# The out stage of three token groups as seven block products, in a fused linear attention and bilinear FFN kernel

## The chip, the cores and the metric

The kernel runs on one core of a Trainium2 chip. The core has TensorE (matmuls, called PE in the profile), VectorE (DVE), ScalarE (ACT), GpSimd (POOL) and the DMA queues, here almost all of them issued by SyncE (SP). Each engine takes its own instructions in the order in which the program lists them, and waits at an instruction until what it needs is there. The metric is the device time of one execution in microseconds (us), as the median of several runs.

## The reference

An attention without softmax, in blocks with a decaying state, feeds a feed-forward layer of two products. Cut to what matters:

```python
# q, k, v: (4 batches, 8 heads, 768 positions, 64); block = 64; lam: one number per head
for b in range(nb):
    intra = (qb @ kb.T * Dmask) @ vb               # Dmask[i, j] = lam ** (i - j) for i >= j, else 0
    inter = (qb * lam_pow) @ kv_state
    out[block b] = intra + inter
    kv_state = lam ** block * kv_state + (kb * rev_pow).T @ vb
x = out as (3072 tokens, 512)
y = ((x @ w_a) * (x @ w_b)) @ w_out                # w_a, w_b: 512 x 1536; w_out: 1536 x 512
```

Everything comes in and goes out as fp32. The kernel computes its matmuls in bf16 with fp32 sums.

## The kernel before, in words

**Units and groups.** The attention works in 24 units of 128 tokens (six per batch). GROUPS (L28) gathers them into eight groups of 4, 1, 2, 4, 4, 4, 4 and 1 units for the feed-forward layer. While TensorE does the layer for one group, the attention of the next group's units is put between its matmuls.

**Attention of a unit.** q and k are scaled by powers of lam and cast to bf16 (`scale`, L317, mostly on GpSimd), transposed by the DMA engines (`dma_start_transpose`, L346) or, for units 4 to 6, on TensorE (`piece_T`); v is cast to bf16 (`make_vb`, on an engine that the table VB_ENG names). `piece_S` makes the scores kq = k q (L374) and `mask` multiplies them by a triangle on VectorE (L391). `pieces_O` sums state times q and v times masked scores into o_ps (L408); `evac_o` copies it as bf16 into xT (L431), the transposed input of the next group. `piece_V` and `kv_beside` bring the state up to date, and KV_ENG says who copies it. The first four units are packed together ahead of group 0.

**The order of the work.** PLAN (L43) is written out by hand. Each group's matmul loop calls `hook(slot)` at fixed points, and PLAN lists what is emitted there: T transpose, S scores, O output, V state, P (PK, PV) preparing a unit, C cast of a w_out chunk, WS a weight sum, X the x sums, W a store of an early output that was kept. `pump` (L230) issues loads on SP's queue, in one order, as far as buffers and LOOKAHEAD allow; transposes and stores are issued on the same queue.

**Weights.** Chunks of fp32 weights of 512 KB land in the pool wst (eight buffers of 4 KB per partition) and are cast to bf16 by `cast_w`. The same pool holds first q and k of units 0 to 3, later the kept outputs, and later still the fp32 copies and oab of the groups 3 to 6. Group 0 uses w_a and w_b in steps, as they land.

**Groups 3 to 6** (`ffn_z`, L625). Here the products x w_a and x w_b are made as 2 x 2 blocks with seven products instead of eight (the Strassen-Winograd scheme): sums of weight blocks are made once (`weight_sum`, on VectorE), sums of x blocks per group (`x_sums`, z_add, z_sub, z_mix, on VectorE). A loop over n = 0..5 (NP = 6 pairs of 128 columns of w_a and w_b) makes seven `product`s of four matmuls of 256 columns each, into the PSUM accumulators U, V and W; U alternates between banks 0 and 1, V between 2 and 3, W is in 4. An accumulator is used for more than one product, so in between ScalarE copies it away (`snap`, L647: u1, v1, u2) and later VectorE subtracts that copy from the accumulator into oab (L679, L688, L689). `finish` of pair n, called in iteration n + 1, adds the last product, has ScalarE copy U into oab (L656), and has VectorE multiply a by b into ab (L658).

**Out stage.** For these groups `out_part` multiplies ab by w_out: four tiles of 128 tokens, twelve chunks of 128 rows, 512 columns each, which is 48 matmuls (L697) per group. ScalarE copies each tile's result (L552) and SP stores it. Groups 0, 1, 2 and 7 go through `ffn` (L510 the products with w_a and w_b, L537 their product, L557 the out stage). Group 7 is one unit, and its output is stored in three parts at the end.

Of the kernel before, what the change touches and what calls it, by code (L numbers as in the profile page):

```python
# [22 lines left out]
def _bc(ap, dims):  # L23
# [8 lines left out]
W_BUFS = 8  # L32
# [10 lines left out]
PLAN = {  # L43
# [21 lines left out]
}  # L65
Z_GROUPS = (3, 4, 5, 6)
KV_ENG = dict(enumerate(["dve"] * 10 +
                        ["act"] * 2 +
                        ["dve"] +
                        ["act"] * 3 +  # L70
                        ["dve"] * 6 +
                        ["act"] +
                        ["dve"]))
VB_ENG = dict(enumerate(["pool"] * 7 +
                        ["dve"] * 3 +
                        ["act"] * 2 +
                        ["dve"] +
                        ["pool"] * 4 +
                        ["dve"] +
                        ["pool"] * 2 +  # L80
                        ["act"] +
                        ["dve"] +
                        ["pool"] * 2))
# [3 lines left out]
def kernel(  # L87
# [25 lines left out]
    wst_pool = ctx.enter_context(tc.tile_pool(name="wst", bufs=W_BUFS))  # L113
    ld_pool = ctx.enter_context(tc.tile_pool(name="ld", bufs=4))
    prep_pool = ctx.enter_context(tc.tile_pool(name="prep", bufs=6))
# [3 lines left out]
    a_pool = ctx.enter_context(tc.tile_pool(name="a", bufs=4))  # L119
# [5 lines left out]
    sum_pool = ctx.enter_context(tc.tile_pool(name="sum", bufs=1))  # L125
    ctx.enter_context(tc.manual_schedule())
# [24 lines left out]
    def load_x(w, u):  # L151
        b, nb = divmod(u, NB)
        t = ld_pool.tile([128, H, D], F32, name=w + "f", tag=w + "f")
        nc.sync.dma_start(out=t, in_={"q": qr, "k": kr, "v": vr}[w][b, nb])  # L154
        raw[u, w] = t
# [7 lines left out]
    staged = {}  # L163
    w_off = [sum(W_CHUNKS[:i]) for i in range(len(W_CHUNKS) + 1)]
# [7 lines left out]
    def load_w(kind, c):  # L172
        t = wst_pool.tile([128, 1024], F32, name="wst", tag="wst")
        if kind == "o":
            t = t[:].rearrange("p (k n) -> p k n", k=2)
# [8 lines left out]
        staged[kind, c] = t  # L184

    def cast_w(kind, c, eng):
        t = staged.pop((kind, c))
# [4 lines left out]
        if eng == "act":  # L192
            nc.scalar.copy(dst, t)
        elif eng == "first":
            nc.vector.tensor_copy(dst[:, :3, :128], t[:, :3, :128])
            nc.gpsimd.tensor_copy(dst[:, 3:, :128], t[:, 3:, :128])
            nc.gpsimd.tensor_copy(dst[:, :, 128:], t[:, :, 128:])
        else:
            nc.vector.tensor_copy(dst, t)  # L199
# [3 lines left out]
    wz = {kind: sum_pool.tile([128, 4, 2, HF], BF16, name="wz_" + kind, tag="wz_" + kind)  # L203
          for kind in "ab"}

    def weight_sum(i):
        kind, j = "ab"[i % 2], i // 2
        w, z = (wa_sb if kind == "a" else wb_sb), wz[kind]
        a11, a12 = w[:, 0:2, :HF], w[:, 2:4, :HF]
        a21, a22 = w[:, 0:2, HF:], w[:, 2:4, HF:]  # L210
        if j == 0:
            nc.vector.tensor_sub(z[:, 0], a22, a21)
        elif j == 1:
            nc.vector.tensor_sub(z[:, 1], a11, z[:, 0])
        elif j == 2:
            nc.vector.tensor_sub(z[:, 2], a12, z[:, 1])
        else:
            nc.vector.tensor_add(z[:, 3], a11, a21)
# [11 lines left out]
    def pump():  # L230
        while pending:
            kind, c = pending[0]
            if kind in "abo":
                if len(staged) >= W_BUFS:
                    return
# [8 lines left out]
    idle_sb = singles.tile([128, 512], BF16, name="idle_sb")  # L244
# [11 lines left out]

    x4 = {}
# [666 lines left out]
```

## Time and profile before

| | us |
|---|---|
| median of 3 runs | 228.15 (227.94 to 228.88) |
| profiled execution | 228.72 |
| its span, first to last instruction | 227.0 |
| TensorE busy in the span | 217.8 |
| VectorE, ScalarE, GpSimd busy | 154.6, 117.0, 59.2 |
| groups 3 to 6 in the span | 85.0 to 215.4 |

The 40 digits of a slice row are tenths of busy time in stretches of 5.7 us. The chain of waits follows the execution back from its last instruction, from each step to what released it; its columns are start, length, and engine, tile and line, with a number of instructions. Rows of instructions by tile give shortest, median and longest duration in ns. Matmuls are pipelined: each lasts longer (379 ns for 512 columns) than the distance to the next one (about 216 ns).

### The profile page before, as it was taken

What the parts mean: (1) busy time and instruction counts of PE and PEld (TensorE: products, weight loads), DVE (VectorE), ACT (ScalarE), POOL (GpSimd) and SP (SyncE); (2) the same over time, 40 slices, a digit from 0 to 9 for tenths busy, and PEclk for the clock granted to TensorE, in tenths of its full rate; (3) what the DMA queues carried; (4) which work ended last, traced back from release to release, by engine and by line L of the source; (5) the groups of instructions that cost most, each with busy time, mean ns of one, the idle gap of its engine ahead of it and who ended that gap; (6) DMA issues with size and microseconds to landing.
All of it is one profiled execution on the core that took longest, in us unless ns stands there. A gap on an engine that the chain in (4) does not pass through costs nothing.

```text
span 227.0 us, 5349 instructions
## 1 busy us (share of the span) xinstructions
PE 217.8 (96%) x2127; PEld 148.3 (65%) x2127; DVE 154.6 (68%) x257; ACT 117.0 (52%) x233; POOL 59.2 (26%) x73
## 2 busy tenths in 40 slices
PE   7798999999899999999999999999999999999994
PEld 2374444447678758877458887448887458885493
DVE  0994773969959868999356988676988318773050
ACT  2685465037443267656247685127576236672261
POOL 6061000147843254424424434460000000000000
PEclk9999999999999999999999999999999999999999
DMA  4999999999999999999999999943020030000311
GB/s 131 318 261 350 359 387 319 271 222 196 233 192 200 240 187 269 212 233 184 181 247 237 205 186 231 169 153 92 3 48 1 27 144 18 1 3 0 141 46 46
DMA packets 97544, 39.40 MB, mean 174 GB/s; under 512 B 85488, under 2 KB 92016, under 8 KB 97520
## 3 DMA queue, kind: packets, MB, share of 16 engines
q1 hardware_dynamic: 97232, 39.00, 80.4%
q8 instruction: 16, 0.26, 0.5%
q10 hardware_dynamic: 288, 0.07, 0.1%
q14 instruction: 8, 0.07, 0.1%
HBM read 28.32 MB, written 6.29 MB: 152 GB/s over the span
## 4 chain that ended last, share of the span: by engine, by line
PE 77%; DMA 8%; SPq 6%; DVE 4%; issue 2%; ACT 1%; ACTq 0%; DVEq 0%
PE op L697 18%; PE U L641 15%; PE b_ps L510 9%; PE op L557 9%; PE a_ps L510 7%; PE V L641 7%; PE o_ps L408 4%; DMA wst<-in_moe_w_b_dram 4%; PE W L641 4%; SPq L154 3%; DMA qkT<-qk 3%; PE kq L374 2%; DMA q<-in_q_dram 2%; PE kvd L438 1%; SPq L183 1%
## 5 line engine op out<-in xcount | busy, mean ns | idle before, releaser
L697 PE MATMUL op<-wo_sb,ab 128*128 128x512 bf16 x192 | 43.3, 379 | 0.0
L391 DVE TENSOR_TENSOR m<-kq,lotri 128x512 bf16<-128x512 f32 x47 | 29.7, 681 | 13.7 <-PE kq L374 13.6
L647 ACT COPY u<-U 128x512 f32<-128x512 f32 x48 | 27.8, 587 | 18.7 <-PE U L641 17.9
L318 POOL TENSOR_TENSOR qk<-kf,lp_k 128x512 bf16<-128x512 f32 x18 | 19.7, 1096 | 53.2 <-DMA kf<-in_k_dram 51.0
L537 DVE TENSOR_TENSOR ab<-a_sb,b_ps 128x128 bf16<-128x128 bf16 (+2 forms) x48 | 19.3, 415 | 20.9 <-ACT a_sb L519 13.6
L697 PEld LDWEIGHTS <-ab 128*128 128x128 bf16 x192 | 18.2, 98 | 20.7
L318 POOL TENSOR_TENSOR qk<-qf,lp_q 128x512 bf16<-128x512 f32 x20 | 24.8, 1239 | 23.0 <-DMA qf<-in_q_dram 23.0
L510 PE MATMUL b_ps<-xT,wb_sb 128*128 128x128 bf16 (+2 forms) x192 | 27.6, 272 | 1.2 <-DVE wb_sb L199 1.0
L510 PE MATMUL a_ps<-xT,wa_sb 128*128 128x128 bf16 (+2 forms) x200 | 27.7, 268 | 0.0
L552 ACT COPY o_sb<-op 128x512 f32<-128x512 f32 (+2 forms) x21 | 11.1, 547 | 31.3 <-PE op L697 28.8
L658 DVE TENSOR_TENSOR ab<-oab 128x1024 bf16<-128x1024 bf16 x24 | 18.8, 783 | 9.1 <-ACT oab L656 9.0
L519 ACT CAST a_sb<-a_ps 128x128 bf16<-128x128 f32 (+2 forms) x48 | 17.2, 376 | 13.1 <-PE a_ps L510 11.5
L557 PE MATMUL op<-wo_sb,ab 128*128 128x512 bf16 (+2 forms) x120 | 22.5, 337 | 0.2 <-DVE ab L537 0.2
L510 PEld LDWEIGHTS <-wb_sb 128*128 128x128 bf16 x192 | 15.8, 98 | 7.7 <-DVE wb_sb L199 1.5
L641 PEld LDWEIGHTS <-wz_a 128*128 128x128 bf16 x192 | 18.3, 98 | 3.3 <-issue 0.3
L510 PEld LDWEIGHTS <-wa_sb 128*128 128x128 bf16 x200 | 16.0, 98 | 6.7 <-DVE wa_sb L199 0.4
L641 PEld LDWEIGHTS <-wz_b 128*128 128x128 bf16 x192 | 18.7, 97 | 2.2
L688 DVE TENSOR_TENSOR oab<-U,v 128x512 bf16<-128x512 f32 x24 | 16.4, 683 | 3.4 <-PE U L641 2.6
L641 PE MATMUL U<-xT,wz_a 128*128 128x256 bf16 x96 | 18.3, 272 | 0.0
L641 PE MATMUL U<-xT,wz_b 128*128 128x256 bf16 x96 | 18.3, 272 | 0.0
L679 DVE TENSOR_TENSOR oab<-W,u 128x512 bf16<-128x512 f32 x24 | 16.3, 681 | 0.9 <-PE W L641 0.9
L431 ACT CAST xT<-o_ps 128x512 bf16<-128x512 f32 (+1 forms) x24 | 12.2, 556 | 9.0 <-PE o_ps L408 8.9
(96 smaller groups left out, 337.0 us busy)
## 6 DMA issues: line engine op xcount, KB each, us to landing
vf<-in_v_dram SPq DMA_DIRECT2D x24, 256.0 KB, 5.0
qf<-in_q_dram SPq DMA_DIRECT2D x20, 256.0 KB, 5.1
kf<-in_k_dram SPq DMA_DIRECT2D x20, 256.0 KB, 5.4
out_dram<-o_sb SPq DMA_DIRECT2D x18, 256.0 KB, 2.2
wst<-in_moe_w_a_dram SPq DMA_DIRECT2D x6, 512.0 KB, 8.4
wst<-in_moe_w_b_dram SPq DMA_DIRECT2D x6, 512.0 KB, 9.0
wst<-in_moe_w_out_dram SPq DMA_DIRECT2D x6, 512.0 KB, 9.1
out_dram<-o_kept SPq DMA_DIRECT2D x5, 256.0 KB, 4.6
```

Source lines behind the costliest of these rows:

```text
L318: eng_of(eng).tensor_mul(dst.rearrange("p (c b) d -> p b c d", b=2), x[:].rearrange("p (b c) d -> p b c d", b=2), lp.rearrange("p (b c) o ...
L391: nc.vector.tensor_mul(m, kq[i], lotri_bc)
L510: nc.tensor.matmul(ps[:, lo:hi], lhsT=w_sb[:, s, f * 128:(f + 1) * 128], rhs=xT[:, s, lo:hi], start=(s == 0), stop=(s == KS - 1), skip_gro ...
L519: nc.scalar.copy(a_sb[:, :gt], ps[:, :gt])
L537: nc.vector.tensor_mul(ab[:, f, :gt], a_sb[:, :gt], ps[:, :gt])
L557: nc.tensor.matmul(op[:, lo:hi], lhsT=ab[:, f, t * 128:(t + 1) * 128], rhs=wo_sb[:, f, lo:hi], start=(f == 0), stop=(f == FC - 1))
L641: nc.tensor.matmul(ps[:, k, :], lhsT=wt[:, s, n * 128:(n + 1) * 128], rhs=rhs[i][:, s, :], start=(fresh and k == 0 and s == 0), stop=True, ...
L647: nc.scalar.copy(t, ps)
L658: nc.vector.tensor_mul(ab[:].rearrange("p (h i) (t c) -> p h i t c", h=2, t=2)[:, :, n], o5[:, :, :, 0, :], o5[:, :, :, 1, :])
L679: nc.vector.tensor_sub(oab[:, 2], W, d["u1"])
L688: nc.vector.tensor_sub(oab[:, 1], d["U"], v1)
L697: nc.tensor.matmul(ops[t][:].rearrange("p a b -> p (a b)"), lhsT=ab[:, f, t * 128:(t + 1) * 128], rhs=wo_sb[:, f, :], start=(f == 0), stop ...
```

## The change

The out stage of groups 4, 5 and 6 is made as 2 x 2 blocks too, with seven products instead of eight. ab (1536 x 512 tokens) is split in halves of chunks and halves of tokens, w_out in halves of rows and halves of columns. A product is then twelve matmuls of 256 columns (6 chunks, 2 token tiles), emitted as two halves (`out_half`, plan entry H), 14 per group. It needs

- four sums of ab blocks per group, each emitted in two parts of 128 x 768 elements (`ab_sum`, entry SM); one of them is written over a block of ab. SUM_ENG puts 11 of the 24 on VectorE and 13 on GpSimd;
- five sums of w_out blocks, once (`out_sum`, entry WO), four on VectorE and one on GpSimd;
- two accumulators (banks 3 and 4), three copies by ScalarE and three subtractions by VectorE per group, and four stores of two token tiles by 256 columns.

The halves of group g are emitted in the loop of group g + 1, which has three hooks per iteration now instead of two: those of group 4 in group 5, of 5 in 6, of 6 in 7. In groups 5 and 6 ("joined") the order within an iteration changes: W comes last and shares bank 2 with V. The last product of the last pair (`fin`) is emitted inside the next group. Group 3 keeps the plain out stage (`out_plain`).

Further: the pool wst is gone, and weights are staged in places that other tiles use later (xT, oab, ab, the sums' buffers); the buffers for loads are 3 instead of 4, for prepared units 5 instead of 6. The first chunk of w_b is cast in two halves of 128 columns on VectorE ("cols"), the second by VectorE and ScalarE together ("both"). Three w_out casts, the last weight sum, and the x sums of groups 5 (two of three) and 6 (all) go to GpSimd. Seven of the scores' halves are copied by ScalarE to SBUF as bf16 first and masked from there (MASK_ACT). State copies of later units go to ScalarE, and v is cast by other engines (VB_ENG). PLAN is new throughout.

```diff
 PLAN (groups 5 to 7 of the new one)
+    5: [(0, 'SM', (4, 1)), (1, 'H', (4, 0)), (1, 'V', 19), (2, 'O2', (19, 20)),
+        (2, 'H', (4, 1)), (3, 'SM', (4, 3)), (4, 'H', (4, 2)), (5, 'S', 21), (5, 'V', 21),
+        (6, 'S', 22), (6, 'H', (4, 3)), (7, 'SM', (4, 5)), (7, 'H', (4, 4)),
+        (8, 'H', (4, 5)), (9, 'P', 23), (9, 'H', (4, 6)), (9, 'SM', (4, 6)),
+        (10, 'SM', (4, 7)), (10, 'H', (4, 7)), (11, 'H', (4, 8)), (11, 'S', 23),
+        (12, 'H', (4, 9)), (12, 'SM', (5, 0)), (12, 'H', (4, 10)), (13, 'SM', (5, 2)),
+        (13, 'H', (4, 11)), (14, 'O2', (21, 22)), (16, 'H', (4, 12)), (17, 'X', 6),
+        (17, 'H', (4, 13)), (17, 'SM', (5, 4))],
...
+    7: [(0, 'H', (6, 0)), (0, 'SM', (6, 1)), (0, 'H', (6, 1)), (0, 'SM', (6, 3)),
+        (0, 'SM', (6, 5)), (0, 'H', (6, 2)), (1, 'H', (6, 3)), (3, 'H', (6, 4)),
...
+SUM_ENG = {(3, 0): 'dve', (3, 1): 'dve', (3, 2): 'pool', (3, 3): 'dve', (3, 4): 'pool', (3, 5): 'pool', (3, 6): 'dve', (3, 7): 'dve', (4, 0): 'dve', (4, 1): 'pool', (4, 2): 'pool', (4, 3): 'pool', (4, 4): 'dve', (4, 5): 'pool', (4, 6): 'pool', (4, 7): 'pool', (5, 0): 'dve', (5, 1): 'dve', (5, 2): 'pool', (5, 3): 'pool', (5, 4): 'dve', (5, 5): 'pool', (5, 6): 'pool', (5, 7): 'dve', (6, 0): 'pool', (6, 1): 'dve', (6, 2): 'pool', (6, 3): 'dve', (6, 4): 'dve', (6, 5): 'pool', (6, 6): 'dve', (6, 7): 'dve'}
...
 cast_w
+        elif eng == "both":
+            nc.vector.tensor_copy(dst[:, :, :128], t[:, :, :128])
+            nc.scalar.copy(dst[:, :, 128:], t[:, :, 128:])
+        elif eng == "cols":
+            nc.vector.tensor_copy(dst[:, :, :128], t[:, :, :128])
+            nc.vector.tensor_copy(dst[:, :, 128:], t[:, :, 128:])
...
 ffn_z, the loop
         for n in range(NP):
+            oab = oab_pool.tile([128, 4, 2, 256], BF16, name="oab", tag="oab")
+            U = z_bank("U", pairs[0] % 2)
+            pairs[0] += 1
+            product(U, n, 1, True)
+            u1 = snap(U)
+            if joined:
+                if fin:
+                    fin.pop()()
+                hook(3 * n)
+            X = z_bank("V", 2 if joined else 2 + n % 2)
+            product(X, n, 4, True)
+            v1 = snap(X)
+            if not joined:
+                hook(3 * n)
+                W = z_bank("W", 4)
+                product(W, n, 0, True)
+                nc.vector.tensor_sub(oab[:, 2], W, u1)
+            product(U, n, 5)
+            u2 = snap(U)
+            if not joined and fin:
+                fin.pop()()
+            hook(3 * n + 1)
+            product(X, n, 6)
+            if joined:
+                nc.vector.tensor_sub(oab[:, 3], X, u2)
+            product(U, n, 3)
+            nc.vector.tensor_sub(oab[:, 1], U, v1)
+            if not joined:
+                nc.vector.tensor_sub(oab[:, 3], X, u2)
+            hook(3 * n + 2)
+            if joined:
+                W = z_bank("W", 2)
+                product(W, n, 0, True)
+                nc.vector.tensor_sub(oab[:, 2], W, u1)
+            fin.append(lambda n=n, U=U, oab=oab: last_product(n, U, oab))
...
 ab_sum (SM)
+        a11, a12 = ab[:, lo:hi, :256], ab[:, NP + lo:NP + hi, :256]
+        a21, a22 = ab[:, lo:hi, 256:], ab[:, NP + lo:NP + hi, 256:]
+        z1, z3 = z[:, 0, lo:hi], z[:, 1, lo:hi]
+        eng = eng_of(SUM_ENG[g, i])
+        if j == 0:
+            eng.tensor_add(z3, a11, a21)
+        elif j == 1:
+            eng.tensor_sub(a21, a22, a21)
+        elif j == 2:
+            eng.tensor_sub(z1, a11, a21)
+        else:
+            eng.tensor_sub(z1, a12, z1)
...
 out_half (H)
+        p, h = O_ORDER[i // 2], i % 2
...
+        c = "U" if p in (1, 5, 3, 2) else "V"
+        fresh = h == 0 and p in (4, 1, 0)
+        if fresh:
+            d[c] = z_bank("op", 3 if c == "U" else 4)
+        ps = d[c]
+        for n in range(h * NP // 2, (h + 1) * NP // 2):
+            for t in range(2):
+                nc.tensor.matmul(ps[:, t, :], lhsT=lhs[p][:, n, t * 128:(t + 1) * 128],
+                                 rhs=rhs[:, n, :], start=fresh, stop=True, skip_group_check=True)
+                fresh = False
+        if h:
+            if p in (4, 1, 5):
+                d[{4: "v1", 1: "u1", 5: "u2"}[p]] = snap(ps)
+            else:
+                o = o_pool.tile([128, 2, 256], F32, name="o_sb", tag="osb")
+                if p == 2:
+                    nc.scalar.copy(o, ps)
+                else:
+                    nc.vector.tensor_sub(o, ps, d[{6: "u2", 3: "v1", 0: "u1"}[p]])
...
+                nc.sync.dma_start(out=rows.rearrange("t p n -> p t n"), in_=o)
```

More of the change, by code (lines that the diff above doesn't have):

```diff
@@ L163, with sum_tile @@
     staged = {}
+    HN, NP = d_model // 2, FC // 2
+    def sum_tile(shape, dt, name, tag):
+        return sum_pool.tile(shape, dt, name=name, tag=tag)
+    ab_stage = ab_pool.tile([128, 3, 1024], F32, name="wst", tag="ab")
+    slots = [lambda: oab_pool.tile([128, 1024], F32, name="wst", tag="oab")] * 2
+    slots += [lambda i=i: ab_stage[:, i] for i in range(3)]
+    slots += [lambda t=t: sum_tile([128, 1024], F32, "wst", t) for t in ("zab", "wy0", "wy1")]
+    once = lambda: xT_pool.tile([128, 1024], F32, name="wst", tag="xT")
+    slots.insert(0, once)
     w_off = [sum(W_CHUNKS[:i]) for i in range(len(W_CHUNKS) + 1)]
@@ L183, in load_w @@
             nc.sync.dma_start(out=t, in_=w_part(r, c))
-        staged[kind, c] = t
+        staged[kind, c] = t, slot
     def cast_w(kind, c, eng):
-        t = staged.pop((kind, c))
+        t, slot = staged.pop((kind, c))
+        if slot is not once:
+            slots.append(slot)
         if kind == "o":
@@ L233, in pump @@
             if kind in "abo":
[L234 removed]
+                if not slots:
                     return
@@ L255, with new_xT @@
                                                 ap=[[0, 128], lam.ap[0]]))
+    gx, xTs = {}, {}
+    g_u0 = [sum(GROUPS[:i]) for i in range(len(GROUPS))]
+    def new_xT(g):
+        gx[g] = xT_pool.tile([128, KS, 512], BF16, name="xT", tag="xT")
+        for i in range(GROUPS[g]):
+            xTs[g_u0[g] + i] = (gx[g], i * BLK)
+    new_xT(0)
     x4 = {}
@@ L501, in pieces_O @@
             kv_copy(us[1], kv["ps"], KV_ENG[us[1]])
-    g_u0 = [sum(GROUPS[:i]) for i in range(len(GROUPS))]
     out_r = out.rearrange("(t p) n -> t p n", p=128)
@@ L691, in ffn_z, with out_plain @@
+        if g not in ZO_GROUPS:
+            out_plain(u0, ab, hook)
+        elif own:
+            fin.pop()()
+            for i in range(14):
+                hook(3 * NP + i)
+    def out_plain(u0, ab, hook):
         early = [f for f in range(FC) if f % NP < NP - 1]
@@ L724 @@
     warm(13, 512)
-    new_xT(0)
-    scr = [ab_pool.tile([128, FC, 512], BF16, name="scratch", tag="ab") for _ in range(2)]
+    scr = [sum_pool.tile([128, FC, 512], BF16, name="scratch", tag="wz_" + kind) for kind in "ab"]
     xs4 = {"q": scr[0][:, 0:4, :], "k": scr[1][:, 0:4, :]}
@@ L847 @@
     cast_w("a", 1, "dve")
-    cast_w("b", 0, "dve")
+    cast_w("b", 0, "cols")
     used["u"] = n0
+    if N_LATE:
+        late_stage = sum_pool.tile([128, 3, 1024], F32, name="wst", tag="wz_a")
+        slots += [lambda i=i: late_stage[:, i] for i in range(N_LATE)]
     pump()
@@ L890 @@
             bank["held"] = set(range(5))
-            ffn_z(g, g_u0[g], gx.pop(g), hook)
-        else:
-            bank["held"] = set()
+            joined = any(name == "H" and us[0] < g for slot, name, us in PLAN[g])
+            own = any(slot >= 18 for slot, name, us in PLAN[g])
+            ffn_z(g, g_u0[g], gx.pop(g), hook, joined, own)
+        else:
+            bank["held"] = {3, 4} if fin else set()
+            if fin:
+                fin.pop()()
             ffn(g_u0[g], n, gx.pop(g), hook, g == 0, g + 1 == len(GROUPS))
```

240 lines of the change are left out of this document (133 added, 107 removed), and 49 rows, old and new, of the table PLAN.

## The prediction

> **What bounds the kernel now.** I read the page's busy rows and slices first, to see which engine is full and where.
>
> ```profile
> span 227.0 us, 5349 instructions
> PE 217.8 (96%) x2127; PEld 148.3 (65%) x2127; DVE 154.6 (68%) x257; ACT 117.0 (52%) x233; POOL 59.2 (26%) x73
> ...
> PE   7798999999899999999999999999999999999994
> ...
> POOL 6061000147843254424424434460000000000000
> PEclk9999999999999999999999999999999999999999
> DMA  4999999999999999999999999943020030000311
> ```
>
> TensorE is full from the fifth slice (22.7 us) on but for a dip in the eleventh, at full clock; GpSimd has nothing to do after 153 us; the DMA engines are full for the first 26 slices, to 148 us. The chain of waits then says at what pace TensorE runs, and where something else is on the path.
>
> ```profile
> 13.61 8.15 DMA wst<-in_moe_w_b_dram
> 21.79 0.70 DVE wb_sb L199
> 22.54 1.04 PE b_ps L510 x4
> ...
> 92.38 5.74 DMA qkT<-qk
> 98.16 0.40 PE kq L374 x8
> ...
> 137.48 0.73 DVE ab L658
> 138.21 0.55 issue
> 138.76 0.27 DVE oab L688
> ...
> 157.12 0.87 PE U L641 x8
> ...
> 175.61 9.71 PE op L697 x45
> ```
>
> A matmul of 512 columns takes 9.71/45 = 0.2158 us, one of 256 takes 0.87/8 = 0.109 us: the price goes with the columns. Three places are not TensorE: the first chunk of w_b (22 us), a transpose by DMA (98 us), and VectorE at 137 us. For the last I looked at what VectorE's product of a and b meets, by tile and in the GpSimd timeline.
>
> ```profile
> L658 DVE TENSOR_TENSOR ab<-oab x24: 674/692/1355, 91.1 to 206.5; 128x1024 bf16<-128x1024 bf16 x24
> ```
>
> ```profile
> L688 DVE TENSOR_TENSOR oab<-U,v x24: 676/683/693, 88.8 to 204.5; 128x512 bf16<-128x512 f32 x24
> ```
>
> ```profile
> 137.25 1.05 POOL L318 TENSOR_TENSOR qk<-kf,lp_k 128x512 bf16<-128x512 f32 x1 [4.37 <-DMA kf<-in_k_dram]
> ```
>
> The product has both inputs in SBUF and takes 692 ns at the median, 1355 at most; the subtraction, with one input in PSUM, never leaves 676 to 693. The longest product began at 137.48, beside a GpSimd scaling that ran from 137.25 to 138.30, and ended 0.53 us after it: it stood still until GpSimd was done.
>
> **The change, part by part** (us on TensorE's path; bounds in brackets).
>
> *Out stage of groups 4 to 6.* Each loses 48 matmuls of 512 columns, 48 x 0.2158 = 10.36, and gets seven products of twelve matmuls of 256, 84 x 0.109 = 9.16 to 9.18. Three groups: -3.54 [-3.6, -3.5]. The weight load of 98 ns stays under the 109 ns. The Trainium skill (TensorE: Matmul & The Clock Gate, Back-to-back issue gap) gives a sustained 131 ns for N=512 and 81 ns for N=128; by these figures, an estimate, the plain stage would take 48 x 0.131 = 6.3 and the products at least 84 x 0.081 = 6.8, so that the change would lose. The 45 matmuls in 9.71 us contradict it here, so it gets no chance of its own.
>
> *Evacuations and stores.* Four copies on ScalarE (0.59 each) become three copies kept for later and one to the output, on VectorE three subtractions (0.68) are new. The four stores per group stay four of 256 KB, in rows of 1 KB; the last is out some 3 us before TensorE ends (one 128-column pair of products and 36 matmuls, 2.66, come after it), so the tail of 3.2 us behind the last matmul stays. 0.
>
> *Sums of w_out.* Five of 1536 elements: on VectorE 0.95 each (the rows of the weight sums), on GpSimd 1536 x 1.04/512 = 3.1. They run in group 3's out stage, where VectorE has only masks. The x sums of group 4 move behind them to the last slot; VectorE runs ahead of TensorE there. 0 [0, +0.7].
>
> *First chunks of w_b.* The cast of 0.70 at 21.79 becomes two; the first half-width one takes about 0.42 (VectorE's fastest 512-element cast of v, 0.41), so b_ps starts 0.27 earlier. The next chunks landed 0.7 to 1.7 us ahead of use, which covers the gain. -0.27 [-0.3, 0].
>
> *Groups 0 to 2.* Units 4 to 6 are prepared in other slots, staging has more places, three w_out casts and the last weight sum go to GpSimd. TensorE idled 1.4 us in 40 to 66 us (25.7 against 24.3 busy). Loads can start earlier, as fewer wait for a staging place. Against it, the scaling of k of unit 5 on VectorE moves from slot 35 to 29, about 47 us, when q of that unit had just landed (GpSimd waited for it until 47.5); masks of unit 4 queue behind it. And transpose, scores and output of unit 6 follow in slots 11 to 13 with 1.3 us of w_out matmuls between each. -0.3 [-1.4, +2.0].
>
> *Transposes and SP's queue, groups 2 and 3.* Unit 13's scores began as the transpose landed. The scores of unit 12 come after 1.7 iterations of group 3, about 91.5 us instead of 92.1, where two weight loads already waited 0.8 for transposes; unit 13's come 2 us later than now. SP issues two kept stores earlier, loads have three buffers instead of four, and GpSimd's weight sum of 3.1 falls between units 8 and 9; GpSimd waited up to 7.7 us for k there, which covers it. +0.3 [-0.3, +2.0].
>
> *Plain stages gone.* TensorE's gaps at 139.3, 142.0 and 195.8 (0.24, 0.18, 0.3) belong to the old order. -0.4 [-0.7, 0].
>
> *Groups 5 and 6 with the previous group's products in their loop.* An iteration is seven products of 0.437 and two or more half products of 0.655. The W and V accumulators share a bank: W waits for V's subtraction, the next V for W's. Let the previous iteration's last matmul be issued at f. ScalarE's copy and VectorE's product of a and b are done at f + 1.4 (0.16 drain, 0.59, 0.69). TensorE needs 0.437 x 3 + 0.655 = 1.97 to finish V, so VectorE subtracts it from f + 2.2 to f + 2.85, and W's turn comes at f + 3.06, after one more product and one half. That is 0.8 and then 0.2 us of cover, gone once VectorE's product stands still for over 1 us behind a GpSimd sum, with both subtractions queued behind it. Such a sum (768 elements) is not in the trace: 1.04/512 and 1.16/512 per element give 1.56 to 1.73; VectorE's eleven are hidden at about 0.55 each (692 ns for 1024). GpSimd works some 60% of group 5 and 30% of group 6. If a product meets a sum at any point of it, it loses over 1 us in 0.6 x 0.4 of cases in group 5, 0.3 us beyond the cover on average: 0.5, in group 6 half; the sums that VectorE itself does are held as well, about 0.45. I take +1.2 [0, +4.8]: the upper end is twelve iterations at the 0.4 us (0.24 + 0.18) that the one held product at 137.48 cost TensorE. The low end is nearer: of the products of groups 3 and 4, run beside GpSimd, five took 0.99 to 1.35, and only that one delayed TensorE. At the joins a VectorE sum of the first halves waits for a GpSimd sum issued just before it, which has nothing else ahead of it by then. Unit 23's scaling on GpSimd stands behind three sums, done some 13 us into group 5, and its transpose (4.8 at the median) ends before its scores, at 20 us: covered.
>
> *x sums of group 6 on GpSimd, in slot 17 of group 5.* They wait for xT of units 21 and 22 (0.92 of matmuls, drain, a queued copy of 0.59: about 1.95 after slot 14 starts), and take 2560 elements, 5.2 to 5.8: z_mix is ready at 7.2 to 7.8. TensorE needs it after 0.9 + 0.3 of output, ten products, two halves and unit 23's output, at about 7.9. Held by three VectorE products (0.5 each) it is late. +0.6 [0, +1.5].
>
> *Handover to group 7.* Its second half product needs the last product of a and b: 0.16 + 0.59 + 0.69 and gaps behind the last matmul, about 1.6, with 0.44 + 0.655 of cover. +0.6 [+0.3, +1.5].
>
> Masks, state copies and v casts that change engine are off the path: ScalarE 52% busy gains some 8 us, VectorE loses as much.
>
> Sum: -3.54 - 0.27 - 0.3 + 0.3 - 0.4 + 1.2 + 0.6 + 0.6 = -1.8. The profiled execution took 228.72 (span 227.0 and 1.7 around it), so 226.9 for it; the median of the three runs is 0.57 lower, so **226.3**.
>
> **Rivals.**
>
> *GpSimd holds VectorE (slower).* Every iteration of groups 5 and 6 meets a sum and loses the 0.4 of 137.48: 4.8 instead of 1.2, x sums 1.5, handover 1.0. Time 226.3 + 3.6 + 0.9 + 0.4 = 231.2. For it: the held product, and sums half again as long as the scaling that held it. Against it: the five held products of groups 3 and 4 cost TensorE 0.4 in all. It decides from 0.35 us per iteration on (1.2 + 12 x 0.25 = 4.2 turns -1.8 into +1.2). The Trainium skill (SBUF — State Buffer, Who interferes with whom) states that a VectorE instruction with two SBUF inputs and a GpSimd one that reads SBUF exclude each other for the whole instruction; the trace agrees, 138.30 against 137.48.
>
> *All cover holds.* GpSimd's sums fall into VectorE's PSUM work: 0.3 for the loop, 0 for x sums, 0.3 for the handover, transposes 0, and 1.0 gained in groups 0 to 2: -3.54 - 0.27 - 0.4 - 1.0 + 0.3 + 0.3 = -4.6, time 223.5. For it: TensorE is at 99% in groups 3 to 6 now, with the same kind of chain.
>
> *Transposes late.* The scores of units 11 to 14 wait, 2.0 instead of 0.3, and units 4 to 6 at their bad end by a little: 226.3 + 1.7 + 0.5 = 228.5, no change. For it: 98.16 and 92.1. Against it: group 3's slots are later for unit 13.
>
> **How the numbers follow.** Forecast 0.42, all cover holds 0.24, transposes late 0.12, GpSimd holds VectorE 0.22. Under 0.5% (1.1 us) a change can't be told from none here. Faster: 0.24 and 0.38 of the forecast, 0.62; same: 0.04 and 0.11, 0.15; slower: 0.22 and 0.01, 0.23. The forecast alone is 225.0 to 227.5. The range takes in the best case with 0.5 below it, and two thirds of the way from 227.5 to the slow case, which leaves out about 0.05 below and 0.15 above: 223.0 to 230.0.
>
> **What would show it.** Half products of 0.655 at 256-column pace, and TensorE's busy total some 3.5 us less. b_ps from 22.3. Products of a and b in groups 5 and 6 at a median near 0.7, a few to 2.3; TensorE waits for VectorE's subtractions summing to about 1. z_mix done within 1 us of its first use. TensorE waiting 0.6 behind group 6. I am wrong if waits for VectorE in groups 5 and 6 pass 4 us, or if scores before 110 us wait for transposes by over 1.5.

## The result

The changed kernel takes 226.69 us (median of 20 executions, 225.31 to 234.54), the kernel before 228.51 (median of 20). Executions over 1.5% longer than the shortest of their kernel, here four above 230 and one of the kernel before, are left out of the ratios; none of the four was traced. The ratio is 0.9912, 95% interval 0.9886 to 0.9937: 2.0 us faster. The profiled execution took 226.41, span 224.7 (before: 228.72, span 227.0). The forecast was 226.3.

The page's busy rows and slices after, against those shown before:

```profile
span 224.7 us, 5609 instructions
PE 214.6 (96%) x2235; PEld 158.8 (71%) x2235; DVE 164.8 (73%) x269; ACT 123.2 (55%) x251; POOL 101.1 (45%) x95
...
PE   7699999989989999999999999899999999999994
...
POOL 6061004256895075541459359786417722052000
```

TensorE is as full as it was (96%) with 3.2 us less to do; GpSimd now works to the 37th slice. The same two groups of VectorE as before, by tile (ns: least, median, most):

```profile
L738 DVE TENSOR_TENSOR ab<-oab x24: 676/692/1525, 91.3 to 204.6; 128x1024 bf16<-128x1024 bf16 x24
...
L769 DVE TENSOR_TENSOR oab<-U,u x24: 676/680/691, 89.2 to 202.6; 128x512 bf16<-128x512 f32 x24
```

The product of a and b still has a median of 692 and one long case, the subtraction from PSUM never leaves 676 to 691. What TensorE waited for behind the start-up (us in total, times, longest):

```profile
PE U L730 <- DVE oab L769: 0.8, 1, 0.8
PE tps L443 <- DVE qk L401: 0.7, 1, 0.7
PE b_ps L596 <- ACT oab L736: 0.5, 1, 0.5
...
PE W L730 <- DVE z_add L706: 0.3, 1, 0.3
```

No row for a transpose by DMA is left (98.16 had one before), and the largest are single events. In the chain the lines for the first chunk of w_b and the out stages are now:

```profile
13.76 7.88 DMA wst<-in_moe_w_b_dram
22.14 3.63 PE b_ps L596 x16
...
164.92 1.31 PE op L852 x12
```

b_ps starts 0.40 earlier (22.54 before), and twelve matmuls of the half products take 1.31, 0.109 each. To see where the 2.3 us of span went, I cut TensorE's time at five starts that both traces have. The last column is the changed kernel once more (experiment e11).

| from ... to (TensorE starts) | before | after | after, again |
|---|---|---|---|
| first a_ps to first b_ps | 4.79 | 3.98 | 3.63 |
| to the out stage of group 0 | 17.60 | 17.28 | 17.27 |
| to group 2 | 24.92 | 24.91 | 24.91 |
| to the first z_mix product of group 3 | 21.68 | 22.21 | 22.18 |
| to that of group 4 | 33.82 | 33.88 | 33.87 |
| to the last matmul | 103.02 | 101.09 | 100.92 |

The first a_ps itself starts 0.41 later after the change (17.75 before, 18.16 after), and what follows the start of the last matmul is 0.27 shorter; with these the table adds up to the 2.3. Five of the six stretches repeat to 0.03 or 0.2 between the two executions of the changed kernel. That is not so of every stretch in every trace: e2 and e4 have the same code up to group 2 and took 26.03 to it in place of 24.91. The last stretch is steady: six traces with the same code from its start on took 100.88 to 101.09, so there terms show that the whole time, with its spread of some 2 us, does not resolve. Of the kernel before there is one trace. In the last stretch, taking from each gap between matmul starts the duration that its shape has in these traces (0.2158 for 512 columns, 0.109 for 256) leaves what TensorE lost there: 1.73 before, 3.37 after. By this account the matmuls themselves fell from 101.29 to 97.72, by 3.57 (the count is the code's, the price of each shape is measured), and new waits gave 1.64 of it back. I call this remainder the lost time below.

### The profile page after: what moved, and what is told of

Its sections match the earlier page's. It is cut to its first block, busy times and chain, and to the rows that moved or that the text cites. A ratio compares the mean times of both kernels' runs of the same rounds, so it can differ in the third digit from the quotient of the medians.

```text
span 224.7 us, 5609 instructions
## 1 busy us (share of the span) xinstructions
PE 214.6 (96%) x2235; PEld 158.8 (71%) x2235; DVE 164.8 (73%) x269; ACT 123.2 (55%) x251; POOL 101.1 (45%) x95
## 4 chain that ended last, share of the span: by engine, by line
PE 80%; DVE 6%; DMA 6%; ACT 3%; issue 2%; SPq 1%; ACTq 0%; DVEq 0%
PE U L730 17%; PE op L852 12%; PE b_ps L596 9%; PE op L643 8%; PE V L730 8%; PE a_ps L596 8%; PE op L792 5%; PE W L730 4%; DMA wst<-in_moe_w_b_dram 4%; PE o_ps L497 3%; DMA k<-in_k_dram 3%; PE kq L457 2%; PE kvd L527 1%; SPq L350 1%; DVE m L480 1%
## 5 line engine op out<-in xcount | busy, mean ns | idle before, releaser
L811 ACT COPY u<-U 128x512 f32<-128x512 f32 x48 | 28.4, 591 | 16.9 <-PE U L730 16.6
L480 DVE TENSOR_TENSOR m<-kq,lotri 128x512 bf16<-128x512 f32 x40 | 25.7, 684 | 3.8 <-PE kq L457 3.6
L596 PEld LDWEIGHTS <-wa_sb 128*128 128x128 bf16 x200 | 16.6, 98 | 6.6 <-issue 0.7
L420 POOL CAST vb<-vf 128x512 bf16<-128x512 f32 x14 | 10.9, 778 | 13.9 <-DMA vf<-in_v_dram 13.9
L769 DVE TENSOR_TENSOR oab<-U,u 128x512 bf16<-128x512 f32 x24 | 16.4, 682 | 0.4 <-PE U L730 0.4
L730 PEld LDWEIGHTS <-wa_sb 128*128 128x128 bf16 x144 | 13.4, 97 | 4.5 <-issue 1.7
L643 PEld LDWEIGHTS <-ab 128*128 128x128 bf16 x120 | 10.1, 98 | 8.6 <-issue 0.3
L736 ACT CAST oab<-U 128x512 bf16<-128x512 f32 x24 | 14.2, 591 | 3.6 <-PE U L730 3.5
```

What stands on the lines that cost most here:

```text
L480: nc.vector.tensor_mul(m, kq[i], lotri_bc)
L596: nc.tensor.matmul(ps[:, lo:hi], lhsT=w_sb[:, s, f * 128:(f + 1) * 128], rhs=xT[:, s, lo:hi], start=(s == 0), stop=(s == KS - 1), skip_gro ...
L643: nc.tensor.matmul(op[:, lo:hi], lhsT=ab[:, f, t * 128:(t + 1) * 128], rhs=wo_sb[:, f, lo:hi], start=(f == 0), stop=(f == FC - 1))
L730: nc.tensor.matmul(ps[:, k, :], lhsT=wt[:, s, n * 128:(n + 1) * 128], rhs=rhs[i][:, s, :], start=(fresh and k == 0 and s == 0), stop=True, ...
L736: nc.scalar.copy(oab[:, 0], U)
L769: nc.vector.tensor_sub(oab[:, 1], U, v1)
```

## The experiments

Each edit is against the changed kernel. Line numbers in the rows of an experiment are those of its own kernel.

### e1: groups 4 to 6 with the plain out stage

```diff
-ZO_GROUPS = (4, 5, 6)
+ZO_GROUPS = ()
```

The entries H, SM and WO are gone from the plan.

> Edit: groups 4 to 6 take the plain out stage again (no half products, no sums of a and b, no sums of w_out); all else as in the changed kernel, 226.7 us. My theory (the terms as forecast): +3.54 for the matmuls, +0.4 for the plain stage's own gaps, and -1.2, -0.6, -0.6 for the joined loop, the x sums and the handover that are not met any more: 1.5 slower than the changed kernel, 228.2. With what the trace of the changed kernel shows in place of the forecasts (0.98 at the join of groups 4 and 5, about 0.6 in the joined loops, 0.66 at the handover, 0 for the x sums): 3.5 + 0.5 - 2.2 = 1.8 slower, 228.5. Rival, all cover holds (the joined loop costs nothing, the change's other parts cost more than forecast): 3.9 slower, 230.6. Rival, the out stage was worth little and the earlier parts brought the gain: less than 0.7 slower. Busy time of TensorE should rise by 3.5 in each of these.

Measured: 233.18, ratio to the kernel before 1.0202 (1.0162 to 1.0242), 6.5 slower than the changed kernel and 2.6 beyond even the rival. The last stretch takes 107.50: matmuls 101.28, as before the change, and 6.22 lost. The waits name the extra losses:

```profile
PE U L700 <- ACT u L781: 1.5, 3, 0.6
...
PE kq L427 <- DVE m L450: 0.8, 1, 0.8
```

The matmul term comes back (101.28 against 97.72 and 97.73 with the products), but as counts times prices it must; what the traces add is that the prices hold: from one out-stage matmul to the next the median is 0.216 in e1 and before the change, 0.109 after it. TensorE's busy total rose by 5.0 (214.6 to 219.6) and not by the 3.5 expected; a matmul lasts longer than the distance to the next, so that short waits count as busy. This kernel does not price the rest: the scores, outputs and x sums of groups 5 to 7 sit in slots that were laid for joined loops, and with plain out stages they collide (scores wait for masks at 161.94, z_mix products for copies of U at 157.66 and 174.56). My expectation took the plain stage's losses from a kernel whose order was made for it. Taking back one part of a change without its order measures both.

### e2: no sums of a and b

```diff
-            lhs[p] = d["z"][:, 1 if p == 6 else 0]
+            lhs[p] = ab[:, :NP, 256:]
```

The entries SM are gone from the plan.

> Edit: the 24 sums of a and b of groups 4 to 6 are left out; the three products that need them read the block a21 in their place, so rows of the output of those groups are not the reference's. Everything else stays, 24 evacuations included. It prices all that the sums cost in the joined loops, whichever engine does them. My theory (VectorE and GpSimd sums are mostly hidden; at the join one VectorE sum of 0.55 stands ahead of a subtraction that TensorE waits for): 0.5 at the join and 0.3 elsewhere, 0.8 faster than the changed kernel's 226.7, 225.9. Rival, GpSimd holds VectorE: each of twelve iterations loses 0.35 or more, 3 to 4 faster, 223. Rival, all cover holds: within 0.3 of 226.7.

Measured: 226.21, ratio 0.9897 (0.9859 to 0.9934). The last stretch takes 100.97, lost 3.24, against 100.92 and 3.19 in e11: leaving out all 24 sums gains nothing. Even the wait at the join of groups 4 and 5 stays (1.07), and TensorE's other gaps in the loops of groups 5 and 6 are those of the changed kernel to 0.02. VectorE and GpSimd at the join:

```profile
141.83 1.25 DVE L708 TENSOR_TENSOR ab<-oab 128x1024 bf16<-128x1024 bf16 x1 [0.40 <-ACT oab L706]
```

```profile
141.50 1.04 POOL L371 TENSOR_TENSOR qk<-kf,lp_k 128x512 bf16<-128x512 f32 x1
```

With no sum ahead of it in GpSimd's queue, a scaling came forward to 141.50 and held VectorE's product, which stood until 142.54 and ended 0.54 later; that took 0.56 more than the usual 0.69, much what the VectorE sum (0.55) had cost at this place. So at the join one delay took the place of another, and e2 does not price the sum there by itself. The rival "GpSimd holds VectorE", 3 to 4 us in the joined loops, is out, and my 0.8 was too much.

### e3: six more sums on GpSimd

```diff
-SUM_ENG: (4,0), (4,4), (5,0), (5,1), (5,4), (5,7) 'dve'
+SUM_ENG: the same six 'pool'
```

> Edit: the six sums of groups 4 and 5 that VectorE did go to GpSimd (group 6 as it was). A dose: six more GpSimd sums of 1.64 in the joined loops, six VectorE sums of 0.55 less. My theory: the join of groups 4 and 5 loses the sum ahead of the subtraction, -0.45; the six added sums each meet a product of a and b for 0.3 beyond the cover in about half the cases, +0.9 at most; together between -0.4 and +0.5 of 226.7. Rival, GpSimd holds VectorE on the path: six times 0.35 or more, +2 or more, 228.7. Rival, all cover holds: -0.45 and nothing else, 226.2.

Measured: 227.01, ratio 0.9938 (0.9912 to 0.9964). The last stretch takes 101.92, 1.0 more than in e11, all of it at two places: 0.36 at 155.17, and the join, where the wait grew from 0.98 to 1.66. VectorE, then GpSimd:

```profile
140.47 1.84 DVE L738 TENSOR_TENSOR ab<-oab 128x1024 bf16<-128x1024 bf16 x1 [0.41 <-ACT oab L736]
```

```profile
140.13 1.63 POOL L825 TENSOR_TENSOR zab<-ab 128x768 bf16<-128x768 bf16 x1
```

The product stood still until 141.76, when GpSimd's sum was done, and then ran its 0.55. At 155.17 a V product waits for the subtraction of W, behind a product that took 1.48 beside two GpSimd sums and masks that took 1.07. The hold is real, but it cost at two places only: about 0.17 for each added sum, half of what the rival needs. My theory erred here too: it expected the join to gain 0.45 from the VectorE sum that left.

### e4: first chunks of w_b cast whole

```diff
-    cast_w("b", 0, "cols")
+    cast_w("b", 0, "dve")
-                    cast_w("b", cs[1], "both")
+                    cast_w("b", cs[1], "act")
```

> Edit: the first chunk of w_b is cast whole on VectorE and the second whole on ScalarE, as before the change. My theory: the first b_ps matmul starts 0.27 later (forecast) to 0.40 later (the two traces: 22.54 against 22.14), and nothing later takes it back: 0.3 to 0.4 slower, 227.0. Rival, a later chunk's landing sets the end of that stage anyway: within 0.1 of the changed kernel.

Measured: 230.13 (median of six, 226.16 to 231.56); the ratio, 0.9896 (0.9841 to 0.9951), rests on two of the six executions and can't resolve 0.3. The profiled execution, of 230.66, shows the cast itself. VectorE's cast of the chunk:

```profile
20.94 0.69 DVE L254 CAST wb_sb<-wst 128x1024 bf16<-128x1024 f32 x1 [0.81 <-DMA wst<-in_moe_w_b_dram]
```

The chunk had landed 0.85 earlier than before the change (21.79), the whole cast ended at 21.63, and b_ps came at 21.92 straight behind a_ps. A half cast saves its 0.27 where the chunk lands late, as in the profiled execution of the changed kernel (21.66, and TensorE stood 0.36). In e2 it landed at 20.74 and a whole cast would have been in time too; in e1 it landed at 21.14, the half cast ended at 21.57, just ahead of b_ps at 21.62, where a whole one of 0.69 would have come some 0.2 too late (an estimate).

Most of what made this execution long is something else, at the start of group 4: VectorE's x sums and GpSimd's sum of w_out met.

```profile
119.09 1.09 DVE L705 TENSOR_TENSOR z_sub<-xT 128x1024 bf16<-128x1024 bf16 x1
120.10 3.57 DVE L706 TENSOR_TENSOR z_add<-xT 128x1024 bf16<-128x1024 bf16 x1
```

```profile
119.60 3.53 POOL L290 TENSOR_TENSOR wy<-wo_sb 128x1536 bf16<-128x1536 bf16 x1
```

TensorE lost 2.31 for z_add and 0.73 for z_mix. In the changed kernel's profiled execution z_mix ended at 119.84 and GpSimd's sum began at 120.27: a margin of 0.4. e8 and e9 go after this.

### e5 and e6: the join and the handover

e5, in the loop of a group:

```diff
             if joined:
-                if fin:
+                if (g, n) != (5, 0):
                     fin.pop()()
-                hook(3 * n)
+                    hook(3 * n)
...
             u2 = snap(U)
...
+            if (g, n) == (5, 0):
+                fin.pop()()
+                hook(3 * n)
```

e6, ahead of group 7:

```diff
             if fin:
                 fin.pop()()
+                bank["next"] = 5
```

> Edit: in the first iteration of group 5 the last product of group 4 is issued after three products of group 5 (its own second and third in between) instead of after one, as the loops of groups 3 and 4 have it. The trace of the changed kernel waits 0.98 there (143.09) for VectorE's subtraction of U, and without any sum of a and b it still waits 1.07. Theory 1: the cover is too short for VectorE's chain at this join (copy of the accumulator on ScalarE, product of a and b, subtraction): with 0.87 more of cover the wait falls to 0.1 or less and the time by 0.7 to 0.9. Theory 2: VectorE as a whole is late there, and the wait moves to the next subtraction (V or W of group 5): less than 0.3 gained.

> Edit: group 7's first accumulators are taken from banks 5 and 6, so that its first b_ps does not come to the bank of the last accumulator of group 6; nothing else. Theory 1 (the wait of 0.66 at the handover is for the bank that ScalarE is still copying): it goes, 0.5 to 0.65 faster. Theory 2 (as the prediction had it: the second half product needs VectorE's last product of a and b, done 0.69 after the copy): the wait moves to the half product and 0 to 0.3 is gained.

e5 measured 225.05, ratio 0.9859 (0.9833 to 0.9885); its last stretch takes 100.55, 0.4 less than in e11. The 0.98 is gone, but the accumulator's copy on ScalarE now keeps the third product waiting (0.40), and a W product waits 0.29 at 146.56. Theory 2 holds for the larger half: the wait moves to other products of the same chain over ScalarE and VectorE. By the ratios the whole time fell by 1.2; 0.4 of that is seen in this stretch, and the rest isn't explained by it.

e6 measured 224.97, ratio 0.9868 (0.9836 to 0.99). Its last stretch takes 100.30, 0.6 less than in e11, and the wait at the handover is gone from the trace. TensorE at the handover in the changed kernel, and ScalarE beside it:

```profile
203.74 0.39 PE L596 MATMUL a_ps<-xT,wa_sb 128*128 128x128 bf16 x4
204.62 0.38 PE L596 MATMUL b_ps<-xT,wb_sb 128*128 128x128 bf16 x4 [0.49 <-ACT oab L736]
204.84 1.47 PE L852 MATMUL op<-wy,ab 128*128 128x256 bf16 x12
```

```profile
203.98 0.59 ACT L736 CAST oab<-U 128x512 bf16<-128x512 f32 x1 [0.41 <-PE U L730]
```

b_ps was given the bank that ScalarE was still reading until 204.57. With another bank the 0.66 goes. The second half product then waits for VectorE's product of a and b, as the prediction had it, but only for 0.07 (at 204.21 in e6, where the product ended at 204.16). Theory 1.

### e7: the second weight sum later

```diff
-    0: ... (18, 'WS', 0), (19, 'WS', 1), ... (23, 'T', 4), ...
+    0: ... (18, 'WS', 0), ... (23, 'T', 4), (23, 'WS', 1), ...
```

> Edit: the second weight sum (wz_b) goes from slot 19 of group 0 to behind the transposes of unit 4 in slot 23. In the trace of the changed kernel it waits 2.5 on VectorE for the last reader of the scratch place that it overwrites (kvd of unit 3, 43.30), and the scaling of k of unit 4 stands behind it, for which TensorE's transposes wait 0.90, and a cast of w_out behind that for 0.36. Theory 1: both go, 1.0 to 1.2 faster. Theory 2 (k of unit 4 had only just landed, or the sum costs as much in its new place): less than 0.3.

Measured: 225.47, ratio 0.9873 (0.9848 to 0.9897). The changed kernel's VectorE queue had been:

```profile
43.73 0.96 DVE L269 TENSOR_TENSOR wz_b<-wb_sb 128x1536 bf16<-128x1536 bf16 x1 [2.48 <-PE kvd L527]
44.60 0.68 DVE L560 TENSOR_TENSOR st<-kvd,bdiag 128x512 bf16<-128x512 f32 x1
45.20 0.68 DVE L401 TENSOR_TENSOR qk<-kf,lp_k 128x512 bf16<-128x512 f32 x1
```

In e7 the 0.90 of the transposes is gone, the 0.37 of the w_out cast stays, and unit 4's outputs now lose 0.74 at 51.6 and 52.2, where a product waits for the masks on VectorE. From the out stage of group 0 to group 2 TensorE took 24.72 instead of 24.91: 0.19 gained. Theory 2 by this stretch; that the time is 0.9 lower than the changed kernel's by the ratios isn't explained by it.

### e8 and e9: the sums of w_out beside the x sums

e8, in the plan:

```diff
-    3: ... (24, 'WO', 2), (25, 'WO', 3), (25, 'WO', 4), (25, 'X', 4)
+    3: ... (20, 'WO', 2), (20, 'WO', 3), (20, 'WO', 4), ... (25, 'X', 4)
-WO_ENG = {..., 2: 'pool', ...}
+WO_ENG = {..., 2: 'dve', ...}
```

e9, in the plan and in out_sum:

```diff
-    3: ... (21, 'P', 18), (24, 'WO', 2), (25, 'WO', 3), (25, 'WO', 4), (25, 'X', 4)
+    3: ... (25, 'WO', 4), (25, 'WO', 3), (25, 'WO', 2), (25, 'P', 18), (25, 'X', 4)
+        if i == 2:
+            x, y = wo_sums[4], wo_sums[6]
```

> Edit: the three last sums of w_out move from slots 24 and 25 of group 3 to slot 20, ahead of the masks of unit 15, and the one that GpSimd did goes to VectorE. The GpSimd sum takes 3.09 and is issued just before the x sums of group 4, which VectorE does from two SBUF inputs; in the profiled execution of the kernel with whole casts the two met, z_add took 3.57 and TensorE stood 2.3 for it, while in that of the changed kernel z_mix ended 0.4 before the GpSimd sum began. Theory 1 (GpSimd holds VectorE here, by chance, a matter of which comes first): z_add stays below 1.6, z_mix is done 1.5 or more before its first use, and no execution is 3 longer than the shortest; where the two don't meet nothing is gained, so the middle of the executions stays within 0.4 of the changed kernel's undisturbed ones. Theory 2 (x sums are late for another reason: the transposes or stores): z_add is late all the same.

> Edit: the meeting of GpSimd's sum of w_out with the x sums of group 4 is forced. GpSimd's sum b11+b22 is worked out from two sums that VectorE has just made (b11-b12 and b12+b22), so that it can't begin before the second of them is done, that is when the x sums begin; the preparation of unit 18 goes behind it. No instruction is added or changed in size. Theory 1 (the hold: a VectorE sum of two SBUF inputs stands still for as long as GpSimd's sum runs): z_sub or z_add takes 2.5 to 3.6 in place of 0.69, the x sums end 2 to 3 later, and TensorE stands 1.5 to 3 at the start of group 4; 2.3 slower than the changed kernel, 228.7. Theory 2 (the hold is no more than the 0.5 to 0.8 that the shorter scalings cost): x sums at most 0.8 later, less than 0.5 slower. Unit 18 comes 2 later in either case, which its scores have some 5 of cover for.

e8 measured 226.4 (225.29 to 227.75), ratio 0.9909 (0.9877 to 0.9941): no change, as theory 1 has it where the two do not meet. But the other half of that theory failed: z_mix was done at 119.47, only 0.06 before its first use (0.58 in the changed kernel, not the 1.5 expected), because VectorE's three sums took 4.38, beside two scalings of 1.77 and 1.75 on GpSimd.

e9 measured 227.79, ratio 1.0001 (0.9972 to 1.0031), 1.8 slower than e11 on the same chip by the ratios. VectorE, then GpSimd, then TensorE:

```profile
116.22 3.58 DVE L678 TENSOR_TENSOR z_add<-xT 128x1024 bf16<-128x1024 bf16 x1
```

```profile
115.78 3.47 POOL L262 TENSOR_TENSOR wy<-wy 128x1536 bf16<-128x1536 bf16 x1 [2.70 <-DVE wy L262]
```

```profile
119.86 0.39 PE L702 MATMUL W<-z_add,wa_sb 128*128 128x256 bf16 x2 [0.72 <-DVE z_add L678]
...
121.04 0.39 PE L702 MATMUL U<-z_mix,wz_a 128*128 128x256 bf16 x2 [0.57 <-DVE z_mix L679]
```

z_add began 0.44 after GpSimd's sum and ended 0.55 after it, and 0.55 is what was left to a product or sum at the end of a hold in e2 and e3 too: it did nothing while GpSimd worked. TensorE lost 1.65 (0.91 and 0.74), and group 4 came 1.53 later than in e11 (35.40 against 33.87). Theory 1, at the low end of its price. In both traces of the changed kernel the 3.1 us GpSimd sum began 0.4 behind the last x sum, and in e4, with the same code at this place, ahead of z_add: nothing in the program fixes which comes first.

### e10 and e11: a mended version, and the changed kernel beside it

e10 has the edits of e6, e7 and e8, and that of e5 in another form, behind the second product of the first iteration of group 5 (the entry H (4, 0) leaves the plan):

```diff
             v1 = snap(X)
+            if (g, n) == (5, 0):
+                out_half(4, 0)
+                fin.pop()()
+                hook(3 * n)
```

> Edits, from what the earlier runs showed: group 7's first accumulators on banks 5 and 6 (0.57 by TensorE's starts in that run); at the join of groups 4 and 5 the first half product of group 4 comes ahead of the last product of a and b, so that VectorE's subtraction has 1.1 more of cover (0.98 waited there, of which moving the last product alone gave 0.33); the sums of w_out all on VectorE and earlier; the second weight sum behind the transposes of unit 4 (0.19). Theory 1 (these waits are separate): 0.57 + 0.8 + 0.2 = 1.6 faster than the changed kernel measured beside it, ratio to the kernel before some 0.984. Theory 2 (VectorE and ScalarE are at their limit around the join and the wait moves again): 0.57 + 0.3 + 0.2 = 1.1 faster.

> The changed kernel itself, beside the two others on one chip. TensorE's time from the first use of z_mix in group 4 to its last matmul should again be 100.9 to 101.1 (it was 101.09, and 100.88 in two kernels with the same code from there on), whatever the start of the execution brings; the time 226.4 or a little under.

e11 measured 226.96 (225.54 to 233.87), ratio 0.9923 (0.9893 to 0.9954); last stretch 100.92. e10 measured 224.93 (224.06 to 225.72), ratio 0.9869 (0.9834 to 0.9905): 1.2 faster than the changed kernel by the two ratios. That is no less than e5 and e6 measured with one edit each (0.9859 and 0.9868), so the whole times don't rank the three; its last stretch is the shortest. It takes 99.97, 0.95 less: 0.57 from the handover and 0.38 from the join, where 0.27 (a U product at 144.18) and 0.37 (W at 146.84) take the place of the 0.98. Theory 2: more cover at one point of the join only moved the wait.

## Why the prediction was right, and where

The time was right (226.3 against 226.69), and the largest term was right in size and in mechanism. The smaller ones were not, one by one: several were right in size for reasons other than those given, and that their sum came out is in part luck, since the joined loop cost 0.6 more than forecast and groups 0 to 2 about 0.5 more, while the x sums cost 0.6 less and the transposes, the plain stages and the handover some 0.6 less together.

*Out stage of groups 4 to 6* (-3.54): 101.29 to 97.72 in the last stretch, -3.57. The sustained rate of the Trainium skill (TensorE: Matmul & The Clock Gate, Back-to-back issue gap), 131 ns for 512 columns, is contradicted by this result as it was by the rows: 216 ns for 512 columns, 109 for 256, and a gain where the estimate from that rate was a loss.

*Evacuations and stores* (0): next to nothing. At 149.91 a product stood 0.14 for a copy of U that ScalarE had queued behind an out-stage copy (148.78).

*First chunks of w_b* (-0.27): right in size where the chunk lands late. b_ps started 0.40 earlier (22.54 to 22.14), of which the landing brought 0.13 (21.79 to 21.66) and the half cast the 0.27 that is left. The other 0.41 by which the first stretch is shorter is no gain: a_ps, where it begins, started that much later. Whether the change or chance moved landing and start, one trace of the kernel before can't tell.

*Groups 0 to 2* (-0.3): the stretches after the first b_ps give -0.32, -0.01 and +0.5, so +0.2 and no gain in this execution; the third is +0.07 in seven of the other kernels with the same code there, +0.27 to +0.53 in e3, e7, e10 and e11. The +0.5 here is mostly a hold that I hadn't priced: z_add of group 3 took 1.09 (from 84.97, 0.68 in e2) beside a cast of v on GpSimd that ended at 85.51, again 0.55 before z_add did, and a W product stood 0.5 at 86.11. The risk that I had named was misplaced. I feared for unit 5's scaling of k behind masks; it was unit 4's, behind a weight sum that waited 2.48 for the scratch place that it overwrites. I had costed the moved scaling's queue and not the memory that the instruction ahead of it writes into. At group 2 TensorE loses 0.92 for unit 6's output, as feared, but the kernel before lost as much in other places.

*Transposes and SP's queue* (+0.3): +0.06 (33.82 to 33.88), and the DMA wait at unit 13 is gone. Covered, as the profile of before had suggested.

*Sums of w_out* (0, at most +0.7): 0 in the profiled execution, but the upper bound was wrong. I priced VectorE's part and forgot that the one sum given to GpSimd runs next to the x sums: +1.53 when they meet in e9, +3.04 in the execution of e4. The mechanism that I looked for in groups 5 and 6 sat here. The Trainium skill (SBUF — State Buffer, Who interferes with whom) has a VectorE instruction with two SBUF inputs and a GpSimd one that reads SBUF exclude each other for the whole instruction; e9 agrees (119.80 against 119.25), as do e2 (143.08 against 142.54) and e3 (142.31 against 141.76).

*Groups 5 and 6 joined loop* (+1.2), *x sums of group 6* (+0.6), *Handover* (+0.6), *Plain stages gone* (-0.4): together +2.0, against 1.64 measured (lost time 1.73 to 3.37): the joined loop 1.83, the handover 0.66 where the kernel before had lost 0.21 (at 216.30), so 0.45, the x sums 0, and the plain stages' gaps at 142.2 and 196.0 (0.34 and 0.30) gone, -0.64. One by one they fail more than that says.

- In the joined loop I gave all of the 1.2 to products held by GpSimd (0.5 and 0.25) and to VectorE's own sums (0.45). Of the products only the one at 145.50 (1.52) was held long, and TensorE did not wait for it; with no sums at all (e2) nothing is gained. Inside the loop the cover of about 1 us was enough. Of the 1.83 that the loops lost, 0.98 is one wait at the join of groups 4 and 5, a place that I had costed at nothing; 0.31 at 171.74 is a wait for a copy of U on ScalarE, and the other 0.54, what is left of the sum, small gaps: 0.07 ahead of V products on the shared bank in five iterations, the 0.14 at 149.91, and less. The product before that copy had ended at 170.65, but ScalarE began the copy at 171.10, straight behind the copy of unit 22's state:

```profile
170.32 0.75 ACT L558 CAST st<-kvd 64x256 bf16<-64x256 f32 x2
171.10 0.59 ACT L811 COPY u<-U 128x512 f32<-128x512 f32 x1
```

  ScalarE made that state copy before the change too. By these rows the new order puts it, and two output copies from 169.37 on, just ahead of a copy that TensorE waits for; no experiment took this apart. VectorE at the join, then TensorE:

```profile
141.28 0.69 DVE L738 TENSOR_TENSOR ab<-oab 128x1024 bf16<-128x1024 bf16 x1 [0.40 <-ACT oab L736]
141.89 0.55 DVE L825 TENSOR_TENSOR zab<-ab 128x768 bf16<-128x768 bf16 x1
142.36 0.69 DVE L769 TENSOR_TENSOR oab<-U,u 128x512 bf16<-128x512 f32 x1
```

```profile
143.09 0.38 PE L730 MATMUL U<-z_sub,wa_sb 128*128 128x256 bf16 x2 [0.81 <-DVE oab L769]
```

  Group 4's loop subtracts U at the end of an iteration, group 5's loop wants that U again after one product. My model of f + 1.4 and f + 2.2 was that of an iteration inside the joined loop; the join has the order of the one loop before it and of the other behind it. By these rows about half of the 0.98 is the sum in front of the subtraction, which held it up by 0.47 (141.89 to 142.36), and the rest the short cover; in e2 and e3 a hold took the sum's place.
- The x sums of group 6 cost 0. z_mix was done at 176.6, 8.0 after the outputs of slot 14 began at 168.63 (forecast 7.2 to 7.8), and first used at 176.79, 8.2 after (forecast 7.9): both were later, and a margin of 0.2 was left.
- The handover cost 0.66, about as forecast, but for a bank of PSUM (e6): with the bank free, the product of a and b, to which I had given it, costs 0.07. That the size agreed is luck. I had followed data and not places.

Of the rivals, *All cover holds* was right about the x sums (0), low in the loop (0.3 against 0.85 without the join), and had nothing for the join. *GpSimd holds VectorE* is refuted where it was placed (e2, e3) and shown where it was not (e9). *Transposes late* did not happen.

## What to carry to other kernels

Cut the busiest engine's time at starts that both traces share, and subtract its own instructions by their shapes: where several traces of the same code agreed, it told waits of 0.1 apart that the whole times could not. When instructions move, list for each queue what memory and which PSUM bank the neighbours need, not only whose data. Where one loop hands over to another of a different order, work out the first iteration by itself, and keep long GpSimd sums away from VectorE work whose end is waited for.

## What I had not expected of the hardware

A GpSimd sum can hold VectorE even where the two are only neighbours by chance: in the changed kernel's trace it began 0.4 after the x sums had ended and TensorE lost nothing, in e4's it began 0.5 ahead of z_add and TensorE lost 3.04. And taking away load need not help: without its sums GpSimd ran a scaling earlier, which held the same VectorE product for 0.56 where a VectorE sum had taken 0.55 (e2).
